# First four V loads in pieces of four tokens, spread by 0/1 matmuls, in a kernel of linear attention and an MLP

## The chip, the cores and the metric

The kernel runs on one core of a Trainium2 chip. The metric is the time of one execution on the device in microseconds (us). A core has a matmul engine (TensorE, PE in the profile), three engines for elementwise work (VectorE = DVE, ScalarE = ACT, GpSimd = POOL), SyncE (SP), which here only issues transfers, and 16 DMA engines that move the data.

## The reference

```python
def _attn_ref(q, k, v, f_logit):            # B, H, S, D = 4, 8, 768, 48
    f = 1.0 / (1.0 + np.exp(-f_logit))
    state = np.zeros((B, H, D, D))
    for t in range(S):
        state = f[:, :, t, :, None] * state + np.einsum('bhd,bhe->bhde', k[:, :, t], v[:, :, t])
        y[:, :, t] = np.einsum('bhd,bhde->bhe', q[:, :, t], state)

def _moe_ref(x, w_in, w_out):               # x: 3072 x 384, w_in: 384 x 2048, w_out: 2048 x 384
    h = x @ w_in
    g = np.maximum(0.01 * h, h)
    return g @ w_out
```

A linear attention with a decay per token and channel gives y; y, with heads side by side, is the input x of two matrix products with a leaky ReLU between them. Inputs and the output are float32.

## The kernel before

The sequence is cut into chunks of 128 tokens. A unit is one chunk of one batch with all eight heads, 24 in all; units 0 to 3 are the first chunk of the four batches. Within a chunk the recurrence becomes matmuls: the logarithm of the decay is summed over the tokens by a matmul with a triangular matrix (`gate_pe`), its exponentials scale k (`em`) and q (`a`), and both are turned so that channels lie on partitions. `score_pe` multiplies them, `mask` keeps the lower triangle, `mix_pe` applies scores and carried state to V, and `state_pe` makes the new state. `y_out` copies the result, `x_pe` and `x_out` turn it, and then, for pairs of units, `up` (eight groups), `up_act` (leaky ReLU) and `down` (two halves) run the MLP. Up to the last units, attention of later units is worked in between the MLP of earlier ones.

The first four units take a path of their own (functions with `q_`). f, k and q of the first chunk are loaded four tokens to a partition, in pieces of 768 bytes, and f of all four batches goes through exp (`q_exp_act`) and ln (`q_ln_act`) in two calls, one per half of the heads. `q_gate32` sums it by matmuls with 32 rows, `q_decay_b` takes exponentials, `q_turn_pe` turns k and q, and `q_k_mul` and `q_q_mul` multiply (half of the heads, pair of heads, pair of batches). `q_score_pe`, `q_wf_act` with `q_mask_pool` and `q_mask`, `q_mix_pe`, `q_back_pe` with `q_back_out` (k back to token partitions) and `q_state_dve` follow. V of these units is loaded in the ordinary way: one token to a partition, pieces of 192 bytes, cast by `cast_v`.

The order of all work is written out by hand, step by step, and every engine takes its steps in that order. SP issues nearly all loads, stores and DMA transposes (`turn2_dma` turns k and q of two units, `x2_dma` turns x of two units, for the pairs in `X2`); POOL issues the loads of w_in and w_out. A one-element copy on POOL (`touch`) makes POOL wait until a load has landed. `idle_pe` runs matmuls on a tile of zeros. Eight PSUM banks serve every step; the last number of a step is its bank.

Of the kernel before, what the change touches and what calls it, by code (L numbers as in the profile page):

```python
# [16 lines left out]
def kernel(  # L17
# [89 lines left out]
    nc.vector.memset(fill, 0.0)  # L107
    lfq = [const.tile([128, 4, 4, 64], BF16, name=f"lfq{i}", tag=f"lfq{i}") for i in range(2)]
# [62 lines left out]
    def load_part(u, name, src):  # L171
        c, b = units[u]
        t = raws[f"{name}_raw"][u % R_RAW]
        nc.sync.dma_start(out=t, in_=src[b, :, c * C:(c + 1) * C, :].rearrange("h t d -> t h d"))
        raw.setdefault(u, {})[name] = t
# [24 lines left out]
    X2 = (9, 10, 11)  # L200
# [23 lines left out]
    emT, aT = wide(gTs[GBUFS - 1]), wide(gTs[GBUFS - 2])  # L224
    kTq = [const.tile([128, 2, 4, 128], BF16, name=f"kTq{i}", tag=f"kTq{i}") for i in range(2)]
# [92 lines left out]
    def q_state_pool(b):  # L318
        put_state(b)
# [195 lines left out]
    load_part(0, "v", v)  # L515
    q_exp_act(1)
    load_part(1, "v", v)
    idle_pe(24, 7)
    q_gate32(0, 0, 1, 2, 3)
    touch('k')  # L520
    q_k_cast(V, 0)
    q_ln_act(1)
    q_k_cast(G, 1)
    q_turn_pe(khq, 0, 4)
    load_part(2, "v", v)
    q_decay_b(0, aT, -1.0, 0, 0)
    q_gate32(1, 0, 1, 2, 3)
    q_decay_b(1, emT, 1.0, 1, 0)
    load_w_in(0)
    q_decay_b(0, emT, 1.0, 0, 0)  # L530
    q_decay_b(2, emT, 1.0, 2, 0)
    q_turn_pe(khq, 1, 5)
    q_k_mul(0, 1, 0, 4)
    q_decay_b(1, aT, -1.0, 1, 0)
    load_w_in(1)
    q_decay_b(2, aT, -1.0, 2, 1)
    q_k_mul(0, 0, 0, 4)
    q_decay_b(1, emT, 1.0, 1, 1)
    load_part(3, "v", v)
    q_q_cast(V, 1)  # L540
    q_decay_b(3, emT, 1.0, 3, 1)
    q_decay_b(0, emT, 1.0, 0, 1)
    q_q_cast(V, 0)
    idle_pe(6, 7)
    q_turn_pe(qhq, 1, 6)
    q_decay_b(0, aT, -1.0, 0, 1)
    load_part(4, "f", f_logit)
    cast_v(G, 0)
    q_decay_b(1, aT, -1.0, 1, 1)
    q_k_mul(1, 0, 0, 5)  # L550
    q_turn_pe(qhq, 0, 7)
    q_decay_b(2, aT, -1.0, 2, 0)
    q_k_mul(1, 1, 0, 5)
    q_decay_b(2, emT, 1.0, 2, 1)
    q_q_mul(1, 0, 0, 6)
    q_decay_b(3, aT, -1.0, 3, 1)
    cast_v(G, 1)
    idle_pe(1, 1)
    q_back_pe(1, 0)
    q_q_mul(1, 1, 0, 6)  # L560
    q_decay_b(3, aT, -1.0, 3, 0)
    q_back_pe(0, 1)
    q_q_mul(0, 0, 0, 7)
    q_decay_b(3, emT, 1.0, 3, 0)
    q_back_out(A, 0, 1)
    q_q_mul(0, 1, 0, 7)
    idle_pe(2, 2)
    q_score_pe(1, 0, 2, 3)
    q_back_out(V, 1, 0)
    q_q_mul(1, 0, 1, 6)  # L570
    q_score_pe(0, 0, 1, 0)
    q_wf_act(1, 0, 1, 3)
    q_mask(1, 0, 0, 2)
    state_pe(1, 3)
# [24 lines left out]
    q_q_mul(0, 0, 1, 7)
    idle_pe(5, 1)  # L600
    q_score_pe(1, 1, 1, 3)
    q_k_mul(0, 1, 1, 4)
    up(0, 2, 5)
    q_mask(1, 1, 0, 1)
    q_wf_act(1, 1, 1, 3)
    q_back_pe(3, 2)
    up(0, 1, 6)
    up_act(0, 2, 5)
    q_mask_pool(1, 1, 1)
    q_back_out(V, 3, 2)  # L610
    up(0, 0, 0)
    up_act(0, 1, 6)
    q_score_pe(0, 1, 7, 4)
    up_act(0, 0, 0)
    up(0, 3, 3)
    q_mask(0, 1, 0, 7)
    q_wf_act(0, 1, 1, 4)
    load_part(4, "q", q)
    cast_v(G, 2)
    q_back_pe(2, 1)  # L620
    up_act(0, 3, 3)
    load_w_out(0)
    q_back_out(V, 2, 1)
    idle_pe(1, 0)
    up(0, 4, 5)
    load_part(4, "v", v)
    cast_v(V, 3)
    q_mask_pool(0, 1, 1)
    state_pe(2, 2)
    up(0, 5, 6)  # L630
    up_act(0, 4, 5)
    load_w_out(1)
    q_state_dve(2)
    load_part(5, "f", f_logit)
    q_mix_pe(2, 0)
    state_pe(3, 4)
    up_act(0, 5, 6)
    q_mix_pe(3, 7)
    y_out(V, 2, 0)
    q_state_pool(2)  # L640
    up(0, 7, 3)
    y_out(A, 3, 7)
    q_state_dve(3)
    load_part(5, "k", k)
    gate_exp(4)
    up(0, 6, 1)
    up_act(0, 7, 3)
    q_state_pool(3)
    x_pe(3, 5)
    x_pe(2, 2)  # L650
    gate_ln(4)
    x_out(V, 3, 5)
    x_out(A, 2, 2)
    load_w_out(2)
    up_act(0, 6, 1)
    idle_pe(4, 4)
    gate_pe(4, 6)
    load_w_out(3)
    up(1, 0, 0)
    decay_em(4, 6)  # L660
    decay_a(4, 6)
    up(1, 5, 7)
    k_scale(V, 4)
    up_act(1, 0, 0)
    up(1, 1, 4)
    up_act(1, 5, 7)
    up(1, 2, 3)
    up_act(1, 1, 4)
    load_part(5, "q", q)
    up(1, 6, 5)  # L670
    up_act(1, 2, 3)
    up(1, 3, 2)
    q_scale(V, 4)
    up_act(1, 6, 5)
    up(1, 4, 1)
    up_act(1, 3, 2)
    down(1, 0, 6)
    up_act(1, 4, 1)
    down(3, 0, 0)
    load_part(5, "v", v)  # L680
    turn_pe(4, 7)
    up(1, 7, 4)
    turn_k(A, 4, 7)
    turn_q(V, 4, 7)
    load_part(6, "f", f_logit)
    cast_v(G, 4)
    down(1, 1, 6)
    up_act(1, 7, 4)
    load_part(6, "k", k)
    gate_exp(5)  # L690
    state_pe(4, 3)
    score1_pe(4, 5, 2)
    gate_ln(5)
    put(V, 1, 6)
    load_part(6, "q", q)
    down(0, 0, 1)
    state_dve(4)
    mask(4, 0, 5)
    load_part(6, "v", v)
    gate_pe(5, 7)  # L700
    down(0, 1, 1)
    mask(4, 1, 2)
    decay_em(5, 7)
    load_part(7, "f", f_logit)
    cast_v(G, 5)
    decay_a(5, 7)
    k_scale(V, 5)
    mix_pe(4, 4)
    q_scale(G, 5)
    put(A, 0, 1)  # L710
    load_part(7, "k", k)
    down(2, 0, 6)
    gate_exp(6)
    y_out(V, 4, 4)
    state_pool(4)
    gate_ln(6)
    out_dma(1)
    turn_pe(5, 3)
    down(2, 1, 6)
    turn_k(A, 5, 3)  # L720
    turn_q(V, 5, 3)
    load_part(7, "q", q)
    load_part(7, "v", v)
    x_pe(4, 5)
    cast_v(V, 6)
    gate_pe(6, 2)
    put(A, 2, 6)
    load_part(8, "f", f_logit)
    state_pe(5, 7)
    x_out(V, 4, 5)  # L730
    score1_pe(5, 1, 4)
    decay_em(6, 2)
    state_dve(5)
    down(3, 1, 0)
    decay_a(6, 2)
    k_scale(G, 6)
    gate_exp(7)
    mask(5, 1, 4)
    out_dma(0)
    gate_ln(7)  # L740
# [648 lines left out]
```

## Time and profile before

| | |
|---|---|
| median of 3 runs | 181.87 us (181.64 to 181.93) |
| profiled execution, whole | 182.43 us |
| its span, first to last instruction | 180.7 us |
| mean granted clock of PE | 0.989 |
| busy: PE, DVE, ACT, POOL | 171.3, 87.0, 123.4, 54.8 us |
| matmuls of `up` (L466), `down` (L486) | 64.5, 65.9 us |
| DMA | 112,582 packets, 31.31 MB |

Rows of the timeline give the start and length of an instruction or of several alike (xN), its engine and line, what it writes and reads, and in brackets the idle time before it with what ended it. L142 is `idle_pe`, L150 and L148 are casts and copies of many kinds (DVE and ACT), told apart by their tiles. PEld is the loading of weights, which runs beside matmuls.

### The profile page before, as it was taken

What the parts mean: (1) busy time and instruction counts of PE and PEld (TensorE: products, weight loads), DVE (VectorE), ACT (ScalarE), POOL (GpSimd) and SP (SyncE); (2) the same over time, 40 slices, a digit from 0 to 9 for tenths busy, and PEclk for the clock granted to TensorE, in tenths of its full rate; (3) what the DMA queues carried; (4) which work ended last, traced back from release to release, by engine and by line L of the source; (5) the groups of instructions that cost most, each with busy time, mean ns of one, the idle gap of its engine ahead of it and who ended that gap; (6) DMA issues with size and microseconds to landing.
All of it is one profiled execution on the core that took longest, in us unless ns stands there. A gap on an engine that the chain in (4) does not pass through costs nothing.

```text
span 180.7 us, 4845 instructions
## 1 busy us (share of the span) xinstructions
PE 171.3 (95%) x1912; PEld 137.7 (76%) x1912; DVE 87.0 (48%) x203; ACT 123.4 (68%) x268; POOL 54.8 (30%) x108
## 2 busy tenths in 40 slices
PE   7597899999999999979999999999999999999992
PEld 5375699776788889669778788788785696897872
DVE  7249954044765978176467365670750254100000
ACT  2577689546888998758779669578796382583711
POOL 3074453114455646330421804250532300000000
PEclk9969999999999999999999999999999999999999
DMA  5999999979988999999999999998999962050102
GB/s 151 303 221 192 211 173 228 210 157 202 219 188 180 193 173 199 169 209 254 163 192 218 185 206 144 249 186 172 234 207 205 201 180 44 5 131 0 44 25 109
DMA packets 112582, 31.31 MB, mean 173 GB/s; under 512 B 105008, under 2 KB 111280, under 8 KB 112560
## 3 DMA queue, kind: packets, MB, share of 16 engines
q1 hardware_dynamic: 110640, 27.47, 79.7%
q0 software_dynamic: 1376, 3.15, 9.5%
q10 hardware_dynamic: 544, 0.39, 0.8%
q8 instruction: 15, 0.25, 0.6%
q14 instruction: 7, 0.06, 0.1%
HBM read 25.17 MB, written 4.72 MB: 165 GB/s over the span
## 4 chain that ended last, share of the span: by engine, by line
PE 54%; ACT 0%; issue 0%
PE ps L466 24%; PE ps L486 22%; PE ps L404 2%; PE ps L425 2%; PE ps L491 1%; PE ps L422 1%; PE ps L332 1%; PE ps L456 1%; PE ps L433 1%; PE ps L335 0%; ACT osb L148 0%
## 5 line engine op out<-in xcount | busy, mean ns | idle before, releaser
L486 PE MATMUL ps<-w_out_b,gT 128*128 128x384 bf16 x368 | 65.9, 326 | 0.0
L466 PE MATMUL ps<-xT,w_in 128*128 128x256 bf16 x528 | 64.5, 273 | 1.0 <-DVE xT L150 1.0
L471 ACT ACTIVATE gT<-ps 128x512 bf16<-128x512 f32 x88 | 51.7, 601 | 15.0 <-PE ps L466 12.9
L466 PEld LDWEIGHTS <-w_in 128*128 128x128 bf16 x528 | 56.0, 114 | 3.0 <-issue 1.1
L486 PEld LDWEIGHTS <-gT 128*128 128x128 bf16 x368 | 34.5, 98 | 19.8
L415 DVE TENSOR_TENSOR wm<-ps,ut 128x512 bf16<-128x512 f32 x40 | 25.2, 683 | 13.2 <-PE ps L404 11.6
L148 ACT COPY osb<-ps 128x384 f32<-128x384 f32 (+1 forms) x24 | 11.2, 466 | 21.2 <-PE ps L486 17.3
L316 POOL CAST sb<-sf 64x192 bf16<-64x192 f32 x40 | 14.6, 364 | 22.4 <-PE ps L422 18.9
L358 POOL TENSOR_TENSOR kqh<-q_raw,a_t 128x384 bf16<-128x384 f32 x11 | 10.1, 920 | 20.1 <-ACT a_end L344 6.8
L150 DVE CAST xn<-ps 128x384 bf16<-128x384 f32 x15 | 8.3, 556 | 7.6 <-PE ps L425 4.5
L354 POOL TENSOR_TENSOR kqh<-k_raw,em_t 128x384 bf16<-128x384 f32 x7 | 6.4, 918 | 17.6 <-ACT em_t L339 13.3
L354 DVE TENSOR_TENSOR kqh<-k_raw,em_t 128x384 bf16<-128x384 f32 x13 | 8.6, 658 | 6.6 <-ACT em_t L339 6.3
L339 ACT ACTIVATE em_t<-ps 128x384 bf16<-128x384 f32 x20 | 10.0, 498 | 2.0 <-PE ps L335 1.9
L323 ACT ACTIVATE f_raw<-f_raw 128x384 f32<-128x384 f32 x20 | 10.6, 530 | 1.0 <-DMA f_raw<-in_f_logit_dram 1.0
L150 POOL CAST v_b<-v_raw 128x384 bf16<-128x384 f32 x11 | 6.5, 588 | 15.8 <-DMA v_raw<-in_v_dram 15.8
L326 ACT ACTIVATE lf<-f_raw 128x384 bf16<-128x384 f32 x20 | 10.5, 526 | 0.3
L142 PE MATMUL ps<-fill 128*128 128x256 bf16 x46 | 9.3, 364 | 1.3 <-DVE fill L107 1.3
L342 ACT ACTIVATE a_t<-ps 128x384 bf16<-128x384 f32 x20 | 9.9, 495 | 0.8 <-PE ps L335 0.5
L358 DVE TENSOR_TENSOR kqh<-q_raw,a_t 128x384 bf16<-128x384 f32 x9 | 5.8, 644 | 7.2 <-ACT a_t L342 6.8
L150 DVE CAST v_b<-v_raw 128x384 bf16<-128x384 f32 x13 | 6.5, 503 | 5.3 <-DMA v_raw<-in_v_dram 5.2
L447 POOL TENSOR_TENSOR sf<-sf,a_end 128x192 f32<-128x192 f32 x16 | 8.8, 549 | 0.4
L441 DVE TENSOR_TENSOR sf<-sf,ps 64x192 f32<-64x192 f32 x16 | 5.5, 343 | 5.2 <-PE ps L433 1.8
(83 smaller groups left out, 192.6 us busy)
## 6 DMA issues: line engine op xcount, KB each, us to landing
v_raw<-in_v_dram SPq DMA_DIRECT2D x24, 192.0 KB, 4.4
out_dram<-osb SPq DMA_DIRECT2D x23, 192.0 KB, 3.2
f_raw<-in_f_logit_dram SPq DMA_DIRECT2D x20, 192.0 KB, 4.3
k_raw<-in_k_dram SPq DMA_DIRECT2D x20, 192.0 KB, 4.3
q_raw<-in_q_dram SPq DMA_DIRECT2D x20, 192.0 KB, 4.4
w_in<-in_moe_w_in_dram POOLq DMA_DIRECT2D x2, 768.0 KB, 10.8
w_out_b<-in_moe_w_out_dram POOLq DMA_DIRECT2D x4, 384.0 KB, 6.7
kq<-in_k_dram SPq DMA_DIRECT2D x4, 192.0 KB, 4.8
```

Of the source, the lines that this page charges most:

```text
L148: eng.copy(out=out, in_=in_)
L150: eng.tensor_copy(out=out, in_=in_)
L316: nc.gpsimd.tensor_copy(out=state_b[b][r, :, e * D:(e + 1) * D], in_=state_f[b][r])
L323: nc.scalar.activation(raw[u]["f"], raw[u]["f"], AF.Exp, scale=-1.0)
L326: nc.scalar.activation(lfs[u % R_LF][:, :, 0:D], raw[u]["f"], AF.Ln, bias=1.0)
L339: nc.scalar.activation(em_ts[u % R_EM], bank(bk)[:, 0:H * D], AF.Exp, scale=1.0)
L354: eng.tensor_mul(khs[u % R_KQS][:, :, 0:D], raw[u]["k"], em_ts[u % R_EM])
L358: eng.tensor_mul(qhs[u % R_KQS][:, :, 0:D], r["q"], a_ts[u % R_EM])
L415: nc.vector.tensor_mul(wms[e][u % R_WM], bank(bk).rearrange("p (i n) -> p i n", i=P2), ut[:, None, :].to_broadcast([128, P2, 128]))
L466: nc.tensor.matmul(bank(bk)[:, i * 256:(i + 1) * 256].rearrange("p (a n) -> p a n", a=2), w_in_p[ff // 8][:, kk, ff // 4 % 2, :, ff % 4], ...
L471: nc.scalar.activation(gTs[m % GBUFS][:, 2 * g:2 * g + 2].rearrange("p f a n -> p (f a n)"), bank(bk), AF.Prelu, alpha=0.01)
L486: nc.tensor.matmul(bank(bk)[:, 0:KD], g_part(u)[:, ff, :], w_out_b[:, ff, :], start=(ff == 0), stop=(ff == NF - 1))
```

## The change

V of the first four units is loaded as f, k and q are, four tokens to a partition, by `load_vq` into a tile of the MLP that is not yet in use. `q_v_cast` casts it on POOL, `q_pick` spreads it to one token per partition with a 0/1 matrix (`pick`, made on DVE at the start) by 16 matmuls of 32 rows and 384 columns, and `q_v_out` copies the result out of PSUM. The first loads of f go in halves, the first halves of all batches ahead of the second ones. x of units 16 and 17 (pair 8) is turned by a DMA transpose in place of six matmul transposes and two copies. The whole order of steps is new. In it w_in is loaded behind a `touch` of q, not of k, and its second half first; all four first units are finished up to their output before the first `up`; and exp and ln of unit 4's f (`gate_exp(4)`, `gate_ln(4)`) stand on ACT between casts of the first units.

```diff
-    first_load(nc.scalar, "f", 2)
-    first_load(nc.sync, "f", 0)
-    first_load(nc.sync, "f", 1)
-    first_load(nc.scalar, "f", 3)
+    first_load(nc.scalar, "f", 2, 0)
+    first_load(nc.sync, "f", 0, 0)
+    first_load(nc.sync, "f", 1, 0)
+    first_load(nc.scalar, "f", 3, 0)
+    first_load(nc.sync, "f", 0, 1)
+    first_load(nc.scalar, "f", 2, 1)
+    first_load(nc.sync, "f", 1, 1)
+    first_load(nc.scalar, "f", 3, 1)
...
+    vqb = const.tile([128, H, 4, D], BF16, tag="vqb")
...
-    X2 = (9, 10, 11)
+    X2 = (8, 9, 10, 11)
...
+    vq = gTs[GBUFS - 3].rearrange("p f a n -> p (f a n)").bitcast(FP32)[:, 0:H * 4 * D].rearrange(
+        "p (h j d) -> p h j d", h=H, j=4)
+    pick = gTs[GBUFS - 3].rearrange("p f a n -> p (f a n)")[:, 3072:3584].rearrange("p (i t j) -> p i t j", i=4, j=4)
+    nc.vector.memset(pick, 0.0)
+    eye = const.tile([128, 32], BF16, tag="eye")
+    for b in range(B):
+        r = slice(32 * b, 32 * b + 32)
+        nc.vector.tensor_copy(out=eye[r, :], in_=ident[r, r])
+    for i in range(4):
+        nc.vector.tensor_copy(out=pick[:, i, :, i], in_=eye)
+
+    def load_vq(b):
+        nc.sync.dma_start(out=vq[32 * b:32 * b + 32].rearrange("p h j d -> p h (j d)"),
+                          in_=v[b, :, 0:C, :].rearrange("h (t j) d -> t h (j d)", j=4))
...
+    def q_v_cast(eng, hh):
+        move(eng, vqb[:, 4 * hh:4 * hh + 4], vq[:, 4 * hh:4 * hh + 4])
+
+    def q_pick(bp, *bks):
+        for i in range(4):
+            for w in range(2):
+                b = 2 * bp + w
+                r = slice(32 * b, 32 * b + 32)
+                nc.tensor.matmul(bank(bks[w])[:, 0:H * D].rearrange("p (h d) -> p h d", h=H),
+                                 pick[r, i].rearrange("p t j -> p (t j)"), vqb[r, :, i, :],
+                                 start=(i == 0), stop=(i == 3))
+
+    def q_v_out(eng, b, bk):
+        move(eng, v_bs[b].rearrange("p h d -> p (h d)"), bank(bk)[:, 0:H * D])
```

The new order of the start, up to the first `up`, shortened (the engine is the first argument where there is one; V is DVE, A is ACT, G is POOL):

```
q_exp_act(0) q_ln_act(0) q_exp_act(1) idle_pe(24) q_gate32(0) q_ln_act(1) q_decay_b(1, emT, hh 0)
idle_pe(5) q_gate32(1) q_decay_b(0, emT, hh 0) q_k_cast(V, 0) q_k_cast(G, 1) load_vq(0)
q_decay_b(0, aT, hh 0) q_decay_b(1, aT, hh 0) q_turn_pe(k, 0) q_decay_b(1, aT, hh 1) load_vq(1) q_decay_b(2, aT)
q_turn_pe(k, 1) q_k_mul(0, 0, 0) load_vq(2) q_decay_b(3, emT) q_k_mul(0, 1, 0) q_decay_b(1, emT, hh 1) load_vq(3)
q_decay_b(2, emT) touch('q') q_q_cast(V, 0) load_part(4, "f") q_q_cast(A, 1) q_k_mul(1, 0, 1) load_w_in(1)
idle_pe(10) q_turn_pe(q, 0) ... q_k_mul(1, 1, 1) q_decay_b(0, emT, hh 1) q_k_mul(0, 0, 1) q_turn_pe(q, 1)
q_decay_b(0, aT, hh 1) load_w_in(0) ... q_k_mul(1, 0, 0) q_decay_b(3, aT) q_q_mul (0,0,0) (1,0,0) (1,1,1)
q_v_cast(G, 1) q_q_mul (1,0,1) (0,1,1) (1,1,0) q_v_cast(G, 0) q_k_mul(1, 1, 0) idle_pe(18) q_score_pe(1, 1)
q_q_mul(0, 1, 0) q_score_pe(1, 0) q_q_mul(0, 0, 1) q_wf_act(1, 1) q_pick(0) q_k_mul(0, 1, 1) q_wf_act(1, 0)
q_mask(1, 0) q_score_pe(0, 0) gate_exp(4) q_mask(1, 1) q_back_pe(0) q_v_out(A, 0) q_pick(1) q_mask(0, 0)
q_wf_act(0, 0) gate_ln(4) q_back_pe(3) q_back_out(V, 0) q_score_pe(0, 1) q_v_out(A, 3) q_v_out(V, 2) q_back_pe(1)
q_back_out(A, 3) q_v_out(V, 1) gate_pe(4) q_mix_pe(0) q_wf_act(0, 1) q_mask(0, 1) state_pe(0) q_mix_pe(1)
state_pe(3) y_out(A, 0) q_back_out(V, 1) q_back_pe(2) y_out(A, 1) q_state_dve(0) x_pe(0) q_back_out(A, 2)
state_pe(1) load_w_out(1) x_pe(1) q_mix_pe(2) x_out(A, 0) q_mix_pe(3) x_out(A, 1) state_pe(2) ... idle_pe(3) up(0, 6)
```

The steps after it are the same kinds as before in another order, with 61 fill matmuls in all where there were 46.

More of the change, by code (lines that the diff above doesn't have):

```diff
@@ L661 @@
[L661 to L668, printed above, removed]
+    q_decay_b(1, aT, -1.0, 1, 1)
+    load_vq(1)
+    q_decay_b(2, aT, -1.0, 2)
+    q_turn_pe(khq, 1, 5)
+    q_k_mul(0, 0, 0, 4)
+    load_vq(2)
+    q_decay_b(3, emT, 1.0, 3)
+    q_k_mul(0, 1, 0, 4)
+    q_decay_b(1, emT, 1.0, 1, 1)
+    load_vq(3)
+    q_decay_b(2, emT, 1.0, 2)
+    touch('q')
+    q_q_cast(V, 0)
+    load_part(4, "f", f_logit)
@@ new lines @@
+    mask(10, 0, 7)
+    q_scale(G, 14)
+    y_out(A, 11, 3)
+    cast_v(V, 14)
+    gate_exp(15)
+    state_pool(11)
+    mix_pe(10, 1)
+    gate_ln(15)
+    x_pe(11, 6)
+    state_pe(14, 0)
+    y_out(A, 10, 1)
+    down(7, 1, 2)
+    x_out(V, 11, 6)
+    load_part(15, "v", v)
+    state_pool(10)
+    load_part(16, "f", f_logit)
+    x_pe(10, 5)
+    gate_pe(15, 4)
+    put(A, 7, 2)
+    out_dma(8)
+    state_dve(14)
+    down(9, 0, 3)
+    x_out(A, 10, 5)
+    decay_em(15, 4)
+    decay_a(15, 4)
@@ new lines @@
+    up_act(5, 7, 6)
+    q_scale(V, 16)
+    load_part(17, "v", v)
+    state_pe(16, 7)
+    x_pe(12, 0)
+    load_part(18, "f", f_logit)
+    put(A, 9, 3)
+    down(10, 0, 2)
+    state_dve(16)
+    x_out(A, 12, 0)
+    load_part(18, "k", k)
+    up(6, 0, 1)
+    gate_exp(17)
+    load_part(18, "q", q)
+    up(6, 2, 5)
+    gate_ln(17)
+    up_act(6, 0, 1)
+    up(6, 7, 6)
+    load_part(18, "v", v)
+    up_act(6, 2, 5)
+    score_pe(7, 3, 0, 7, 1)
+    up_act(6, 7, 6)
+    gate_pe(17, 5)
+    out_dma(9)
@@ new lines @@
+    turn2_dma(8)
+    gate_pe(18, 3)
+    up(6, 4, 2)
+    up_act(6, 6, 1)
+    cast_v(V, 18)
+    decay_em(18, 3)
+    down(12, 0, 0)
+    decay_a(18, 3)
+    load_part(19, "v", v)
+    k_scale(V, 18)
+    up_act(6, 4, 2)
+    q_scale(G, 18)
+    state_pe(17, 6)
+    gate_exp(19)
+    down(11, 1, 4)
+    state_dve(17)
+    gate_ln(19)
+    state_pe(18, 7)
+    gate_pe(19, 5)
+    out_dma(10)
+    put(A, 11, 4)
+    x_pe(15, 1)
+    up(6, 5, 3)
+    decay_em(19, 5)
+    x_out(V, 15, 1)
+    decay_a(19, 5)
@@ new lines @@
+    put(A, 17, 4)
+    down(18, 0, 3)
+    down(19, 1, 5)
+    down(18, 1, 3)
+    out_dma(17)
+    put(A, 19, 5)
+    score_pe(11, 1, 0, 6, 2)
+    put(A, 18, 3)
+    up(10, 0, 7)
+    mask(23, 0, 6)
+    up(10, 5, 4)
+    mask(22, 1, 0)
+    up_act(10, 0, 7)
+    up(10, 2, 5)
+    mask(23, 1, 2)
+    up_act(10, 5, 4)
+    up(10, 3, 3)
+    out_dma(19)
+    mask(22, 0, 1)
+    up_act(10, 2, 5)
+    up(10, 1, 6)
+    up_act(10, 3, 3)
+    mix_pe(23, 7)
+    out_dma(18)
+    up_act(10, 1, 6)
+    mix_pe(22, 0)
@@ new lines @@
+    y_out(V, 23, 7)
+    up(10, 4, 4)
+    y_out(A, 22, 0)
+    down(20, 0, 2)
+    x2_dma(11)
+    up_act(10, 4, 4)
+    up(10, 6, 5)
+    up(10, 7, 1)
+    up_act(10, 6, 5)
+    down(21, 0, 3)
+    up_act(10, 7, 1)
+    down(20, 1, 2)
+    down(21, 1, 3)
+    put(A, 20, 2)
+    out_dma(20)
+    up(11, 0, 6)
+    put(A, 21, 3)
+    up(11, 2, 7)
+    up_act(11, 0, 6)
+    out_dma(21)
+    up(11, 6, 0)
+    up_act(11, 2, 7)
+    up(11, 3, 4)
+    up_act(11, 6, 0)
+    up(11, 5, 5)
+    up_act(11, 3, 4)
```

1343 lines of the change are left out of this document (605 added, 738 removed).

## The prediction

> **What bounds the kernel now.** I read the span and the stretches by engine first.
>
> ```profile
> span 180.7 us, 4845 instructions
> ```
> ```profile
> 20.98:77.80 56.82, 56.82 (x694) 46.57 (x692) 31.57 (x67) 45.06 (x102) 25.15 (x45) 1.00 1.05 191
> 77.80:79.20 1.40, 0.36 (x7) 0.27 (x4) 1.37 (x3) 0.48 (x1) 1.14 (x2) 1.00 0.92 198
> 79.20:177.50 98.30, 98.29 (x1022) 79.70 (x1020) 39.97 (x77) 65.15 (x136) 20.14 (x39) 1.00 0.82 156
> ```
>
> The first two numbers of a row are its length and PE's busy time. From 20.98, where the first `up` starts, to its last matmul at 177.5 PE is never idle but for 1.04 us. So the end is: start of the first `up`, plus a fixed amount of matmul work, plus holes, plus 3.2 us of last copy and store. The hole, in the timeline:
>
> ```profile
> 77.55 1.03 DVE L150 CAST v_b<-v_raw 128x384 bf16<-128x384 f32 x1 [1.61 <-DMA v_raw<-in_v_dram]
> 78.61 0.36 DVE L150 COPY xT<-ps 128x384 bf16<-128x384 bf16 x1
> 79.02 0.82 PE L466 MATMUL ps<-xT,w_in 128*128 128x256 bf16 x6 [1.04 <-DVE xT L150]
> ```
>
> A V cast waits for its late load, and the copy of x queued behind it on DVE lets PE stand. The change rewrites the whole order, so three things count: when the first `up` starts, how much work is left then, which holes come.
>
> **Work left.** In the new order units 2 and 3 are done up to their output before the first `up`; now much of them comes after it.
>
> ```profile
> 23.29 0.40 PE L277 MATMUL ps<-qTq,kTq 64*128 64x128 bf16 x8
> ...
> 24.30 0.39 PE L300 MATMUL ps<-ident,kTq 128*128 128x128 bf16 x4
> ...
> 24.52 0.27 PE L142 MATMUL ps<-fill 128*128 128x256 bf16 x1
> ...
> 26.11 0.36 PE L294 MATMUL ps<-v_b,wm 128*128 128x48 bf16 x8
> ...
> 26.32 0.33 PE L433 MATMUL ps<-v_b,kqh 128*128 128x96 bf16 x4
> ...
> 26.48 0.36 PE L294 MATMUL ps<-v_b,wm 128*128 128x48 bf16 x8
> ...
> 26.69 1.48 PE L466 MATMUL ps<-xT,w_in 128*128 128x256 bf16 x12
> ```
>
> Matmuls overlap, so starts count, not durations: turning back .22 (24.30 to 24.52), mix .21, state .16. Moved ahead are two each (1.18), one score block and the gate of unit 4 (estimated at .3 each): 1.8. Five fills (.11 each by 1.48/12 less the drain) vanish: .55. Six transposes of x 16 and 17 go to a DMA transpose: at .055 each (.22 for four) .33. That transpose has cover: its result is wanted 8 us of matmuls after unit 17's mix, so I cost it at nothing; a longer wait on SP would cost only what exceeds that. Left after the first `up`: 156.5 - 1.04 - 1.8 - .55 - .33 = 152.8. Hence span = first `up` + 152.8 + holes + 3.2, and a first `up` at 24.7 without holes breaks even.
>
> **The first `up`, step by step.**
>
> ```profile
> 0.81 0.89 SPq L70 DMA_DIRECT2D fq<-in_f_logit_dram  x2
> 1.74 2.67 SPq L70 DMA_DIRECT2D kq<-in_k_dram  x4
> 4.62 2.93 SPq L70 DMA_DIRECT2D qq<-in_q_dram  x4
> 6.44 0.84 ACT L229 ACTIVATE fq<-fq 128x768 f32<-128x768 f32 x1 [3.39 <-DMA fq<-in_f_logit_dram]
> 8.21 0.63 PE L240 MATMUL ps<-steps,lfq 32*128 32x128 bf16 x32 [1.74 <-ACT lfq L232]
> 9.67 0.37 ACT L245 ACTIVATE gT<-ps 128x256 f32<-128x256 f32 x1
> 9.99 1.73 POOL L190 DMA_DIRECT2D w_in<-in_moe_w_in_dram  x2
> 10.09 1.04 PE L240 MATMUL ps<-steps,lfq 32*128 32x128 bf16 x32
> 11.16 4.25 ACT L245 ACTIVATE gT<-ps 128x256 f32<-128x256 f32 x15 [1.12 <-PE ps L240]
> 14.18 1.41 DVE L263 TENSOR_TENSOR qTq<-ps,gT 128x256 bf16<-128x256 bf16 x4
> ```
> ```profile
> DMA to landing us min/median/max: 3.6/4.1/5.0
> ```
>
> *f in halves.* Loads of f land 3.6 to 5.0 after issue (last row); the last of four whole ones, issued near 1.3, releases ACT at 6.44. Four first halves are as many bytes as the first two whole loads, issued at .81 and landing by some 4.5. So exp starts at 4.6; bounds 4.3 and 5.6 (no gain in latency, 1.3 + 4.3). From exp to the first decay are 3.23 us (6.44 to 9.67): 7.8. Four more issues delay SP and ACT by some .9 each; ACT's table load still ends near 3.9, hidden. Only eight hardware loads can be open in the compiled program (each waits for the eighth before it), so k now waits for first halves of f to land, near 4.0 instead of 1.74. But k's bytes queued behind f's anyway, and q waited for f's landing already; I put q's landing unchanged, at 11.0, with +.6 as bound.
>
> *Decays.* The second gate block writes a bank that the first decay reads: it starts at 8.2 (7.8 + .37) and takes .63 or 1.04, the two rows L240. The trace slowed it:
>
> ```profile
> 5.00:10.00 5.00, 2.80 (x48) 1.74 (x47) 1.06 (x4) 3.50 (x5) 1.28 (x3) 0.97 1.10 309
> 9.70:13.00 3.30, 3.24 (x50) 2.50 (x47) 1.15 (x4) 2.18 (x9) 2.52 (x4) 0.50 1.38 211
> ```
>
> The granted clock (third from last) was .50 from 9.7 to 13, after 5 us in which PE was busy 2.80. The new order has 5 and 10 fills there. The Trainium skill, "TensorE: Matmul & The Clock Gate", Part 1, says that a free-running window of about 3.4 us decides; the trace agrees in that the slow stretch has about that length. By that rule the phase is luck, and half clock may fall elsewhere ahead of the first `up`. I take the full clock, .63, and +.4 as bound. DVE's new constants (about 1.3 us) are free: DVE was busy 1.06 of these 5 us.
>
> Decays run on ACT from 8.9 at 4.25/15 = .283 for 256 columns; eleven such widths precede the products of hh 1, batches 2 and 3: 12.0.
>
> *Products.* DVE does one each .353 (1.41/4). The eleventh, the last that score (1,0) needs, ends at 12.1 + 3.9 = 16.0; q's cast on DVE, 11.1 to 11.7, is not last, nor is the half on ACT. Score .40: 16.5.
>
> *ACT's list.* From there ACT has thirteen operations up to the second copy of x: three casts of scores, exp and ln of unit 4, two V copies, two copies of k, two of y, two of x.
>
> ```profile
> L281 ACT CAST wm<-ps 128x512 bf16<-128x512 f32 x4 | 2.3, 584 | 1.1 <-PE ps L277 1.1
> L148 ACT CAST xn<-ps 128x384 bf16<-128x384 f32 x2 | 0.9, 482 | 1.2 <-PE ps L294 1.2
> L148 ACT COPY kqh<-ps 128x512 bf16<-128x512 bf16 x1 | 0.8, 754 | 0.0
> ...
> L323 ACT ACTIVATE f_raw<-f_raw 128x384 f32<-128x384 f32 x20 | 10.6, 530 | 1.0 <-DMA f_raw<-in_f_logit_dram 1.0
> ...
> L326 ACT ACTIVATE lf<-f_raw 128x384 bf16<-128x384 f32 x20 | 10.5, 526 | 0.3
> ```
>
> 3 x .584 + 6 x .482 + 2 x .754 + .53 + .526 = 7.2, less some .04 of overlap at each: 6.7. DVE's masks and PE's steps between run beside it. First `up`: 23.2; bounds 22.6 and 24.3.
>
> *The spread of V.* The sixteen 0/1 matmuls (32 rows, 384 columns) fall before the first `up`, beside ACT's list. The nearest row, 32 gate matmuls of 32 rows and 128 columns in .63, gives .02 for 128 columns; 16 x 3 x .02 = .95 since there four row groups alternate and here two, up to 1.9 if that halves it. I take 1.3; against ACT's 6.7 it is hidden, and 1.9 would move the first `up` by perhaps .3. The Trainium skill, "TensorEngine Tiling (Array Packing)", Key Properties, speaks against it: a change of tiling mode drains the engine. No row here isolates a drain; by that rule a few of them, an estimated .3 us, would come on top.
>
> *Holes.* V of unit 13 will again be cast close to its load, but no x copy sits directly behind it. Following each other producer I find .4 us or more to spare; the new order is as tight, so I take .6 of holes, bounds 0 and 2.
>
> *Sum.* 23.2 + 152.8 + .6 + 3.2 = 179.8, .9 below the span of 180.7. The profiled execution took 182.43 as a whole; the runs' median is 181.87. Taking .9 off the median: 181.0.
>
> **Rivals.**
>
> *f of unit 4 blocks ACT (slower).* ACT's list holds exp of unit 4 ahead of V copies and score casts, and its load competes with w_in:
>
> ```profile
> q0 software_dynamic: 28, 0.06, 57.5%
> ...
> q0 software_dynamic: 626, 1.25, 95.9%
> q1 hardware_dynamic: 659, 0.12, 16.0%
> ```
> ```profile
> f_raw<-in_f_logit_dram SPq DMA_DIRECT2D x1, 192.0 KB, 13.1
> ```
> ```profile
> q1 hardware_dynamic: 1811, 0.34, 125.0%
> ```
>
> The first row is w_in's queue from 12.2 to 13.0, where its packets begin, 2.3 after its issue at 9.99. The next two are 14 to 21 us: 659 packets on SP's queue against w_in's 626, 94 a microsecond. The last row is 22 to 23.5, w_in done: 1,207 a microsecond. So the same load took 13.1 us in this stretch (middle). In the new order V's larger pieces go first, to 12.5, then the 1,024 packets of f, .85 us, done by 13.4; w_in is issued only when q has landed and a touch on POOL has run (estimated .6, from landing at 11.0), at 11.7, so it moves packets from 14.0. (Its first half, 384 packets at 626 in 7 us, is through by 18.3, the second by 22.6: in time for the first `up`.) ACT wants f at 17. Spared: .6. It decides from the point where w_in starts with over some 210 packets of f still to go. Half of them left: 5.4 us more, f at 20.2, 3.1 late, time 184; all left: up to 6 late, 187. Chance .12.
>
> *New holes (slower).* The new order may meet late loads, or a DMA transpose that holds SP, more often: 2.5 us of holes where I put .6 gives 182.9. For: the 16 DMA engines are full up to some 140 us (slices of 4.5 us, in tenths):
>
> ```profile
> DMA  5999999979988999999999999998999962050102
> ```
>
> Against: V's first four units have a quarter of the packets. Chance .16.
>
> *The start gains nothing (no change).* If half clock, whole-f latency or the spread put the first `up` at 24.2, the gain of the hole remains but is eaten by .6 of holes: 182.0. Chance .15.
>
> **How the numbers follow.** The forecast has .57. A measurement of this kernel can tell about 0.2%, .36 us. Faster .57 (first `up` plus holes below 24.3), the same .13, slower .30 (the two rivals and a little of the third). Range: 22.6 with no hole gives 178.6, thus 179.7; at the upper end 183.2 leaves out most late f's.
>
> **What would show it.** Right: exp at 4.6, decays from 8.9, last product near 17, first `up` near 23.2, PE busy from there to 175.9 + holes, no wait behind V of unit 13. Wrong: ACT idle before f of unit 4; a first `up` beyond 24.7; waits of PE above 1.5 us after it.

## The result, and the profile after

| | before | after |
|---|---|---|
| median | 181.71 us (181.23 to 183.52, 17 runs) | 183.66 us (182.44 to 186.11, 17 runs) |
| ratio, 95% interval | | 1.0083 (1.0054 to 1.0112) |
| profiled execution, span | 182.43, 180.7 us | 182.44, 180.7 us |

The change is slower, by some 1.5 to 2 us; 181.0 was forecast, with faster as the likeliest case. The ratios here and below leave out runs more than 1.5% above the fastest of their kernel (four of after, 185.28 to 186.11; one each of again, fill20 and v_behind; two of fill_qv, 184.06 and 184.21), which the medians and ranges keep. The two profiled executions are equally long and so don't show the loss by themselves: that of before was 0.7 us above the median of its runs here, and that of after was the fastest of its 17. The span of after, and two of its windows, in the columns of the prediction (the last is GB/s):

```profile
span 180.7 us, 4904 instructions
```
```profile
5.00:10.00 5.00, 3.06 (x77) 1.94 (x75) 1.76 (x12) 4.27 (x10) 0.00 (x0) 1.00 0.87 256
24.89:177.50 152.61, 152.42 (x1657) 124.17 (x1655) 67.58 (x139) 107.50 (x235) 43.51 (x81) 1.00 0.92 171
```

From the first `up` at 24.89 to its last matmul TensorE is busy for 152.42 of 152.61 us. So the fixed part came out as worked out (152.8), and all that is to be explained lies ahead of 24.89, where 23.2 had been forecast. The timeline of after up to there:

```profile
3.51 2.68 SPq L70 DMA_DIRECT2D kq<-in_k_dram  x4
4.31 0.84 ACT L250 ACTIVATE fq<-fq 128x768 f32<-128x768 f32 x1 [0.32 <-DMA fq<-in_f_logit_dram]
6.24 2.58 SPq L70 DMA_DIRECT2D qq<-in_q_dram  x4
8.65 2.96 ACT L266 ACTIVATE gT<-ps 128x256 f32<-128x256 f32 x8 [0.67 <-PE ps L261]
8.86 2.75 SPq L243 DMA_DIRECT2D gT<-in_v_dram  x4
10.31 0.56 DVE L155 CAST khq<-kq 128x768 bf16<-128x768 f32 x1 [3.47 <-DMA kq<-in_k_dram]
13.45 0.83 ACT L153 CAST qhq<-qq 128x768 bf16<-128x768 f32 x1 [1.84 <-DMA qq<-in_q_dram]
17.35 1.59 POOL L155 CAST vqb<-gT 128x768 bf16<-128x768 f32 x2 [1.56 <-DMA gT<-in_v_dram]
18.20 1.07 ACT L317 CAST wm<-ps 128x512 bf16<-128x512 f32 x2 [2.87 <-PE ps L313]
19.00 0.82 PE L283 MATMUL ps<-vqb,gT 32*128 32x384 bf16 x8 [0.55 <-POOL vqb L155]
19.16 0.54 ACT L359 ACTIVATE f_raw<-f_raw 128x384 f32<-128x384 f32 x1
24.89 0.82 PE L502 MATMUL ps<-xT,w_in 128*128 128x256 bf16 x6
```

f comes as planned: its first exp at 4.31, and the decays run from 8.65. Then three engines sit idle with a DMA in the brackets: DVE until k is there (10.31), ACT until q is (13.45), POOL until V is (17.35). Before, k's loads were issued at 1.74 and q's at 4.62; now at 3.51 and 6.24. What TensorE waited for, and the chain of waits back to the start (start, length, what):

```profile
PE ps L294 <- DVE khq L155: 2.3, 1, 2.3
PE ps L261 <- ACT lfq L253: 0.6, 2, 0.4
PE ps L283 <- POOL vqb L155: 0.5, 1, 0.5
```
```profile
0.81 2.69 DMA fq<-in_f_logit_dram
...
3.51 0.72 SPq L70
...
10.49 6.70 DMA gT<-in_v_dram
...
17.35 1.61 POOL vqb L155 x2
...
19.00 0.82 PE ps L283 x8
```

The chain starts at a landing of f: SP stands until 3.50, then issues k, q and V one after another, and the last of V's loads, issued at 10.49, takes 6.70 us. With eight loads of f, the first load of k is the ninth; it goes out when the first of the eight has landed. From 19.00, where the V spread begins, the chain is TensorE's own matmuls without a gap up to the first `up`.

### The profile page after: what moved, and what is told of

Same layout as the page of the kernel before. It is cut to its first block, busy times and chain, and to the rows that moved or that the text cites. A ratio compares the mean times of both kernels' runs of the same rounds, so it can differ in the third digit from the quotient of the medians.

```text
span 180.7 us, 4904 instructions
## 1 busy us (share of the span) xinstructions
PE 172.9 (96%) x1937; PEld 139.4 (77%) x1937; DVE 85.6 (47%) x211; ACT 124.0 (69%) x268; POOL 54.0 (30%) x105
## 4 chain that ended last, share of the span: by engine, by line
PE 86%; DMA 5%; SPq 4%; ACT 1%; issue 1%; POOL 1%; DVE 1%; POOLq 0%; DVEq 0%
PE ps L522 33%; PE ps L502 32%; DMA gT<-in_v_dram 4%; SPq L70 3%; PE ps L513 3%; PE ps L440 2%; PE ps L461 2%; PE ps L469 2%; PE ps L368 2%; PE ps L458 2%; DMA fq<-in_f_logit_dram 1%; PE ps L527 1%; PE ps L492 1%; PE ps L403 1%; POOL vqb L155 1%
## 5 line engine op out<-in xcount | busy, mean ns | idle before, releaser
L502 PE MATMUL ps<-xT,w_in 128*128 128x256 bf16 x528 | 62.9, 273 | 0.1
L507 ACT ACTIVATE gT<-ps 128x512 bf16<-128x512 f32 x88 | 51.1, 605 | 9.0 <-PE ps L502 6.9
L153 ACT COPY osb<-ps 128x384 f32<-128x384 f32 (+1 forms) x25 | 11.8, 473 | 22.4 <-PE ps L522 19.6
L394 POOL TENSOR_TENSOR kqh<-q_raw,a_t 128x384 bf16<-128x384 f32 x13 | 12.6, 967 | 28.3 <-ACT a_end L380 13.0
L147 PE MATMUL ps<-fill 128*128 128x256 bf16 x61 | 10.6, 340 | 1.3 <-DVE fill L111 1.3
L155 DVE CAST xn<-ps 128x384 bf16<-128x384 f32 x13 | 7.2, 557 | 8.1 <-PE ps L461 5.3
L147 PEld LDWEIGHTS <-fill 128*128 128x128 bf16 x61 | 7.2, 122 | 3.3 <-DVE fill L111 1.3
L155 POOL CAST v_b<-v_raw 128x384 bf16<-128x384 f32 x6 | 3.0, 504 | 20.8 <-DMA v_raw<-in_v_dram 20.8
L390 POOL TENSOR_TENSOR kqh<-k_raw,em_t 128x384 bf16<-128x384 f32 x5 | 4.9, 979 | 9.7 <-ACT em_t L375 9.7
```

The lines of the kernel that those rows point to most:

```text
L147: nc.tensor.matmul(bank(bk)[:, 0:256], fill[:, 0:128], fill[:, 0:256], start=True, stop=True)
L153: eng.copy(out=out, in_=in_)
L155: eng.tensor_copy(out=out, in_=in_)
L390: eng.tensor_mul(khs[u % R_KQS][:, :, 0:D], raw[u]["k"], em_ts[u % R_EM])
L394: eng.tensor_mul(qhs[u % R_KQS][:, :, 0:D], r["q"], a_ts[u % R_EM])
L502: nc.tensor.matmul(bank(bk)[:, i * 256:(i + 1) * 256].rearrange("p (a n) -> p a n", a=2), w_in_p[ff // 8][:, kk, ff // 4 % 2, :, ff % 4], ...
```

## Experiments

Theories at the start: (1) f in eight loads holds SP back, so that k, q and V land late; (2) half clock ahead of the first `up` costs the time; (3) V's loads themselves are slow. Rows are of one profiled execution of each kernel, times of five rounds against the kernel before on the same chip. There were four chips, on which the kernel before had medians of 181.25 to 181.48 us, so the ratios compare best. The columns q and V give the start of the first step that reads their landed data, with a dash where no step waits for it.

| kernel | q | V | first `up` | span less it | time, range | ratio, interval |
|---|---|---|---|---|---|---|
| before_again | – | – | 20.80 | 158.6 | 181.15, one run | |
| again | 14.77 | 18.75 | 26.30 | 155.7 | 183.7 (182.1 to 184.9) | 1.010 (1.0069 to 1.0131) |
| fill20 | 13.63 | 17.88 | 25.42 | 155.8 | 183.44 (182.4 to 185.4) | 1.010 (1.0069 to 1.0132) |
| f_whole | 11.91 | 15.80 | 24.01 | 156.0 | 181.83 (181.3 to 182.4) | 1.0024 (1.0009 to 1.0039) |
| h1_pool | 13.29 | 17.15 | 24.70 | 156.0 | 182.28 (181.9 to 183.0) | 1.0045 (1.0029 to 1.0061) |
| k_between | 13.32 | 17.44 | 25.93 | 155.8 | 182.96 (181.9 to 183.4) | 1.0078 (1.0051 to 1.0106) |
| v_spread | 11.07 | 13.62 | 24.24 | 156.0 | 181.7 (181.3 to 182.3) | 1.0012 (0.9991 to 1.0032) |
| v_spread_after | 12.76 | 15.33 | 23.36 | 156.0 | 181.43 (180.8 to 182.7) | 1.001 (0.9989 to 1.0032) |
| v_behind | 13.95 | 21.49 | 31.82 | 155.7 | 188.43 (186.5 to 189.6) | 1.0369 (1.0326 to 1.0411) |
| v_ordinary | 11.10 | – | 31.98 | 156.0 | 189.83 (189.1 to 190.1) | 1.0449 (1.0408 to 1.049) |
| touch_k | – | 15.37 | 24.06 | 155.9 | 181.69 (181.2 to 182.1) | 1.001 (0.9988 to 1.0031) |
| x_pe | 11.35 | 15.49 | 24.08 | 156.4 | 182.14 (181.7 to 182.5) | 1.0033 (1.0016 to 1.005) |
| f_whole_fill | 11.59 | 15.71 | 23.51 | 156.0 | 181.37 (181.0 to 181.6) | 0.9999 (0.9986 to 1.0012) |
| v_spread_fill | 10.86 | 13.40 | 23.57 | 155.9 | 181.25 (181.2 to 181.6) | 0.9998 (0.9987 to 1.0009) |
| fill_qv | 11.65 | 15.63 | 23.89 | 156.0 | 181.52 (181.2 to 184.2) | 1.0007 (0.9997 to 1.0018) |

Span less first `up` is 155.7 to 156.0 in every kernel that has the rest of the change (x_pe and before_again have another): the time is the first `up` plus a constant.

**again.** The changed kernel once more, unedited.

> The changed kernel unchanged, for its spread and a second profile. Clock theory: its runs fall into steps by mean granted clock, about 182.5 us at .99 to 1.0, 184 at .98, 185.4 at .972 (one, two, three windows of 3.4 us at half clock), and the kernel before stays near 181.7. Load theory (late loads at the start alone make the loss): times scatter without regard to the clock.

Its profiled execution took 183.72 us, a usual one. The rows of its timeline and waits that answer to those above, and its line by cores:

```profile
14.77 0.83 ACT L153 CAST qhq<-qq 128x768 bf16<-128x768 f32 x1 [3.02 <-DMA qq<-in_q_dram]
18.75 1.60 POOL L155 CAST vqb<-gT 128x768 bf16<-128x768 f32 x2 [1.65 <-DMA gT<-in_v_dram]
26.30 0.81 PE L502 MATMUL ps<-xT,w_in 128*128 128x256 bf16 x6
```
```profile
PE ps L294 <- DVE qhq L155: 2.4, 1, 2.4
PE ps L294 <- DVE khq L155: 1.8, 1, 1.8
PE ps L283 <- POOL vqb L155: 1.0, 1, 1.0
```
```profile
core 0: 182.0 us, clock 1.000
```

Issued at the same times as in after (q 6.24, V 8.87), q is read 1.3 us later and V 1.4 later, and the first `up` comes 1.4 later. The clock was full throughout, while after had this stretch (granted clock third from last):

```profile
10.00:15.00 5.00, 4.01 (x33) 3.17 (x34) 2.85 (x8) 3.16 (x8) 2.70 (x4) 0.70 1.04 225
```

From the reading of q to the first `up` after took 11.44 us and again 11.53, so the slow stretch does not show in the time. Nor do the runs of again fall into steps by their clock: 183.72 us came at 1.0 and 182.12 at .991. Half clock is not the loss: theory 2 falls.

**fill20.** Idle matmuls ahead of k's turning, to keep TensorE busy.

```diff
+    idle_pe(20, 7)
     q_turn_pe(khq, 0, 4)
```


> Twenty more fill matmuls on PE ahead of the turning of k, where PE stood 2.3 us; all else as changed. Clock theory: fewer windows at half clock, mean clock .99 to 1.0 in nearly all runs and the median 1 us or so lower, 182.4 to 182.8. Load theory: no gain, or .3 us slower, as fills can only delay the turning of k.

The clock of its profile stayed at 1.0, and the time did not move against that of again (183.44 and 183.7): TensorE waits for q and V at any clock.

**f_whole.** f in four whole loads; all else as changed.

```diff
-    first_load(nc.scalar, "f", 2, 0)
...
+    first_load(nc.scalar, "f", 2)
+    first_load(nc.sync, "f", 0)
+    first_load(nc.sync, "f", 1)
+    first_load(nc.scalar, "f", 3)
```


> f loaded in four whole loads again, all else as in the changed kernel. Load theory: k is issued near 1.75 instead of 3.51, q lands near 11 instead of 13.35 and V's pieces near 15 instead of 17.2, while exp starts at 6.4 instead of 4.3; products then wait for decays (13.8) instead of q (13.9), so the first up moves little, to 24.3 to 24.9. Time within 0.5 us of the changed kernel by that alone. Clock theory: PE no longer waits 2.3 us for k, so fewer half-clock windows and 1 us or more faster in the median.

```profile
1.74 2.68 SPq L70 DMA_DIRECT2D kq<-in_k_dram  x4
4.50 2.88 SPq L70 DMA_DIRECT2D qq<-in_q_dram  x4
6.27 0.84 ACT L246 ACTIVATE fq<-fq 128x768 f32<-128x768 f32 x1 [3.21 <-DMA fq<-in_f_logit_dram]
11.91 0.19 POOL L187 COPY seen<-qq 128x1 f32<-128x1 f32 x1 [2.19 <-DMA qq<-in_q_dram]
15.80 1.60 POOL L151 CAST vqb<-gT 128x768 bf16<-128x768 f32 x2 [1.49 <-DMA gT<-in_v_dram]
```

k goes out at 1.74 again, q at 4.50, and both q and V are there 1.5 to 3 us sooner than in the changed kernel's two profiles. f's exp starts 2 us later, and yet the time falls by 1.87 us against again, and the range of the runs from 2.8 to 1.0 us. Halving f, which was to bring exp 1.8 us forward, costs that much instead. This misses the expectation as written: late loads alone were to move the time by 0.5 us at most, and 1 us or more was to speak for the clock. But f_whole itself ran at half clock from 10 to 13 us (row below, under f_whole_fill) and again at no time, so the clock did not make this gain. Theory 1 stands, with a larger effect than I gave it.

**before_again.** The kernel before, profiled a second time.

> The kernel before, unchanged, for a second profile. If the hole of 1.04 us behind the cast of V of unit 13 belongs to every execution, PE waits about 1 us there again and the span is 180.4 to 180.7. If it was one execution's luck, the span is 179.2 to 180.1 with PE waiting under .3 us after its first up: the saving of 1.04 in the prediction was then not there to be had.

```profile
span 179.4 us, 4845 instructions
20.80:176.30 155.50, 155.30 (x1716) 126.47 (x1713) 72.40 (x145) 110.39 (x240) 46.71 (x85) 1.00 0.92 171
```

TensorE has no hole here. The 1.04 us behind V of unit 13 belonged to that one execution, not to the kernel. So what a first `up` of the changed kernel must beat is 179.4 - 156.0 = 23.4, not 24.7.

**h1_pool.** The second halves of f through POOL's queue, so that k need not wait.

```diff
+    for b in (0, 2, 1, 3):
+        first_load(nc.gpsimd, "f", b, 1)
```


> The second halves of f are loaded by POOL's queue, which does not count against the eight open loads; all else as changed. Load theory: exp still near 4.3, k issued near 1.75, k lands by 8.6, q by 11, V's pieces by 15; the first up comes at 23.2 to 23.8 instead of 24.89, so 1.1 to 1.7 us faster than the changed kernel's like runs, about 181.2 to 181.9. If the open loads do not matter, the first up stays at 24.9.

```profile
8.46 0.84 ACT L248 ACTIVATE fq<-fq 128x768 f32<-128x768 f32 x1 [2.41 <-DMA fq<-in_f_logit_dram]
```

k goes out at 1.73 and the first exp starts at 4.32, but the second halves, issued from 1.40 to 3.80, release the second exp only at 8.46, and q is read at 13.29. The first `up`, expected at 23.2 to 23.8, comes at 24.70. Of again's loss of 2.2 us 0.8 is left.

**k_between.** k of two batches between the halves of f.

```diff
+    first_load(nc.sync, "k", 0)
+    first_load(nc.sync, "k", 1)
     first_load(nc.sync, "f", 0, 1)
```


> The changed kernel with k of the first two units issued between the first and the second halves of f. If the loads wait for the one eight before them, the third of f's second halves is now the one that waits (at 3.5 us), k's first two go out at once, and q's four go out 0.9 us sooner, at about 5.3 instead of 6.24; the second exponential comes up to 1 us later. If q's landing sets the time through its issue: 182.6 to 183.0. If the second exponential takes over, or the bytes in flight set q's landing and not its issue: 183.4 to 184.

```profile
9.05 0.84 ACT L250 ACTIVATE fq<-fq 128x768 f32<-128x768 f32 x1 [3.00 <-DMA qq<-in_q_dram]
13.32 0.19 POOL L191 COPY seen<-qq 128x1 f32<-128x1 f32 x1 [2.13 <-DMA qq<-in_q_dram]
```

As in the theory of the eighth load before, the wait now falls on a half of f, and q goes out at 5.71 instead of 6.24. But the second exp comes 3 us late, not 1, and q is read hardly sooner. The bracket names q; what exp reads is f, whose last half went out on SP near 3.9, and the longest landing of a half was 5.1 us. 182.96 lies in the range of the first expectation, but not by its mechanism: one wait was exchanged for another.

**v_spread and v_spread_after.** V's pieces to every fourth partition, as k and q go, with whole f and with f in halves. V of the first four units is then in the wrong order of tokens.

```diff
-        nc.sync.dma_start(out=vq[32 * b:32 * b + 32].rearrange(
+        nc.sync.dma_start(out=vq[slice(b, None, 4)].rearrange(
```


> On the kernel with f loaded whole: V's pieces go to every fourth partition of the tile, as those of k and q do, in place of 32 neighbouring ones, so V of the first units comes out in a wrong order; all else equal. If the 32 neighbouring partitions slow V's packets, these take about 41 ns in place of 67 to 79, V's pieces land by 13.5 to 14 instead of 15.7, unit 4's f by 16 and the time falls by up to .3 us, to 181.5. If the slowing has another cause (queues, other traffic), V lands at 15.5 to 16 again and the time stays at 181.8.

Packets, MB and share of SP's queue from 10 to 12 us, and V's loads with their median from issue to landing, first of f_whole, then of v_spread:

```profile
q1 hardware_dynamic: 534, 0.39, 113.7%
```
```profile
gT<-in_v_dram SPq DMA_DIRECT2D x4, 192.0 KB, 5.7
```
```profile
q1 hardware_dynamic: 883, 0.64, 107.5%
```
```profile
gT<-in_v_dram SPq DMA_DIRECT2D x4, 192.0 KB, 3.8
```

With the engines about equally full, a packet takes 1.7 times as long with V going to 32 neighbouring partitions as with V spread; the last of q's packets are in the stretch too. With whole f the time hardly moves (181.7), since V is there before TensorE asks.

> The changed kernel with its f in halves, and V's pieces sent to every fourth partition, as k and q go, instead of 32 neighbouring ones (V of the first four units then comes in the wrong order of tokens). Theory A, that V's slow packets beside q's are what holds q back and spreads the time: in the kernel with whole f the same edit brought V's landing from 5.7 to 3.8 us behind its issue and q's packets in the stretch 10 to 12 us from 534 to 883. Here q would be cast at 12.5 to 13.0 instead of 13.4 to 14.8, V at 15 instead of 17.4 to 18.8, the first `up` at 24.2 and the time 182.4 with a spread under 1 us. Theory B, that the series of issues on SP alone, 1.77 us late, sets q's landing: q cast at 13.4 or later, the time 183.6 with the old spread.

```profile
12.76 0.83 ACT L153 CAST qhq<-qq 128x768 bf16<-128x768 f32 x1 [1.12 <-DMA qq<-in_q_dram]
15.33 1.59 POOL L155 CAST vqb<-gT 128x768 bf16<-128x768 f32 x2 [0.23 <-DMA gT<-in_v_dram]
23.36 0.82 PE L502 MATMUL ps<-xT,w_in 128*128 128x256 bf16 x6
```

With f in halves the same edit takes off 2.3 us against again. The two profiles, both at full clock, add up: q read 2.0 us sooner and TensorE's 1.0 us of waiting for V gone, against 2.94 at the first `up`. So theories 1 and 3 hold together, and the loss needs both parts: k and q issued late (k by 1.77 us), and V's slow loads right behind q. The first `up` and the time came out better than expected (24.2 and 182.4). The spread of runs stayed at 1.9 us, where under 1 was expected.

**v_behind.** V's loads behind f and k of unit 4 instead of right behind q.

```diff
     load_part(4, "k", k)
+    load_vq(0)
+    load_vq(1)
+    load_vq(2)
+    load_vq(3)
```


> The changed kernel, f in halves, with V's four pieces issued behind f and k of unit 4 instead of right behind q. If V's packets hold q back, q is now cast by 12.9 us (13.4 to 14.8 in the changed kernel, 12.8 where V went to spread partitions); V itself lands 1 to 2 us later, at 18.5 to 20. If q's landing is what costs the time, 182.5; if V's own landing ends the chain, the 0/1 matmuls wait until 20 to 21.5 us and the time is 184 to 185.5, slower than the changed kernel.

```profile
13.95 0.83 ACT L153 CAST qhq<-qq 128x768 bf16<-128x768 f32 x1 [2.26 <-DMA qq<-in_q_dram]
21.49 1.59 POOL L155 CAST vqb<-gT 128x768 bf16<-128x768 f32 x2 [5.20 <-DMA gT<-in_v_dram]
23.13 1.46 PE L283 MATMUL ps<-vqb,gT 32*128 32x384 bf16 x8 [4.56 <-POOL vqb L155]
```

q, at 13.95, lies between the changed kernel's two profiles (13.45 and 14.77), with the ordinary loads of unit 4 now behind it. So it is not V alone that holds q back; only V spread out gave 12.76. V itself is 2.7 us later than in again, more than expected. TensorE waits 4.6 us for it and then runs at half clock, so that eight matmuls of the V spread take 1.46 us where they took .82. The time, 188.43, is beyond the 184 to 185.5 expected.

**v_ordinary.** Whole f, V in pieces of 192 bytes as before, no 0/1 matmuls.

```diff
-    load_vq(0)
+    load_part(0, "v", v)
...
-    q_v_out(A, 0, 7)
+    cast_v(A, 0)
```


> On the kernel with f loaded whole: V of the first four units loaded in the ordinary way (1024 pieces of 192 bytes each) and cast where the spread's copies stood; no 0/1 matmuls. If V in larger pieces pays, this is slower: 4096 packets at about 900 a microsecond ahead of unit 4's f and w_in, V landed only by 16 to 23 where w_in's packets alternate, first up 1 to 4 us later, 183 to 186. If the spread costs more than the pieces save, it is faster than 181.8.

ACT's longest wait:

```profile
ACT f_raw L355 <- DMA f_raw<-in_f_logit_dram: 5.9, 1, 5.9
```

189.83, beyond the 183 to 186 expected: f of unit 4 is caught behind w_in, the prediction's first rival, and the first `up` comes at 31.98. From 14 to 17 us w_in's queue moved 227 packets and SP's 96. Half clock follows the wait (.50 from 25 to 31 us) and is in the 8 us that the larger pieces of V are worth in this order.

**touch_k.** Whole f; w_in behind k instead of q.

```diff
-    touch('q')
+    touch('k')
```


> On the kernel with f loaded whole: POOL's touch reads k in place of q, so w_in's load starts some 2 us earlier (10.3 in place of 12.5). By the prediction's first rival w_in's packets then alternate with unit 4's f from 12.6 on, f lands at 19 to 22.5 in place of 16.5 to 17, ACT waits for it 1 to 4 us with the casts of the first units behind it, and the time is 182.8 to 186. If w_in and f do not disturb each other, 181.8.

```profile
9.87 1.73 POOL L191 DMA_DIRECT2D w_in<-in_moe_w_in_dram  x2
```
```profile
DMA packets 1785, 1.12 MB, mean 223 GB/s; under 512 B 412, under 2 KB 1785, under 8 KB 1785
q1 hardware_dynamic: 1785, 1.12, 114.3%
```

w_in is issued at 9.87 and not at 12.45, but from 9 to 14 us all 1785 packets belong to SP's queue. The loss that I expected did not come, and the time is that of f_whole.

**x_pe.** Whole f; x of units 16 and 17 turned by TensorE again.

```diff
-    X2 = (8, 9, 10, 11)
+    X2 = (9, 10, 11)
...
-    x2_dma(8)
     put(A, 13, 6)
+    x_pe(16, 7)
+    x_out(V, 16, 7)
+    x_pe(17, 6)
+    x_out(V, 17, 6)
```


> f in whole loads, and x of units 16 and 17 transposed by TensorE as in the kernel before, with two copies out by VectorE; all else as with whole f. The prediction's term says that the six transposes cost 2 x 0.165 us of a TensorE that has no gaps there: 182.1 against 181.8 with the DMA transpose. If they fit beside VectorE's or ScalarE's work, or the DMA transpose itself costs as much elsewhere, the two are equal within 0.1.

Span less first `up` is 156.4 here and 156.0 with the DMA transpose, so the profile has the term (0.33) at 0.4. The intervals of the times overlap (1.0033 and 1.0024); by them alone it is not settled.

**f_whole_fill, v_spread_fill and fill_qv.** Whole f and 12 more idle matmuls ahead of the first widths; then the same with V spread (wrong order of tokens), and the same with q's second cast on DVE.

```diff
-    idle_pe(24, 7)
+    idle_pe(36, 7)
```
```diff
-    q_q_cast(A, 1)
+    q_q_cast(V, 1)
```


> f in whole loads and 12 more idle matmuls ahead of the first widths matmuls, where TensorE was idle for 1.48 us. If the half clock at 9.96 to 13.4 follows that idle time, the second group of widths matmuls takes 0.65 instead of 1.31 us, k's transposes 1.2 instead of 1.9, and the first `up` comes 0.3 to 0.8 us earlier than 24.0: 181.0 to 181.5, about the kernel before. If the products on VectorE and the exponentials on ScalarE set the chain and TensorE only waits, the first `up` stays at 24.0 and the time at 181.8.

The windows from 10 to 13 us, of f_whole and of f_whole_fill (granted clock third from last):

```profile
10.00:13.00 3.00, 3.00 (x49) 2.68 (x49) 0.96 (x3) 2.10 (x7) 0.74 (x2) 0.50 1.14 199
```
```profile
10.00:13.00 3.00, 2.97 (x64) 2.47 (x52) 1.22 (x3) 2.60 (x8) 1.06 (x2) 1.00 1.12 210
```

Here the clock does count: the first `up` comes at 23.51 instead of 24.01, the time falls to 181.37, level with the kernel before, and the runs lie within 0.65 us. The runs of f_whole say the same: the two of its twelve at a mean clock of 1.0 took 181.32 and 181.37, the others 181.63 to 182.36.

> Whole f, 12 more idle matmuls, V's pieces to every fourth partition (V of the first four units in the wrong order of tokens). Theory: with whole f, V has landed 2 us before TensorE asks for it, so the edit gives nothing: 181.4 as with neighbouring partitions, first `up` at 23.5. Rival: V's faster packets let everything behind them land sooner and show in the time: 181.0 or less.

181.25: nothing gained over f_whole_fill, as the theory had it. At full clock or near it, then, whole f gives 181.37 and 181.25 with V to neighbouring and to spread partitions, f in halves 183.44 (fill20) and 181.43.

> Whole f, 12 more idle matmuls, and the second cast of q by VectorE (0.55 us) instead of ScalarE (0.91 us at 13.16, between the exponentials that VectorE then waits for, 1.10 us). If ScalarE's list sets the first scores, they come 0.4 to 0.9 us sooner, the first `up` at 22.6 to 23.1 and the time is 180.5 to 181.0, below both kernels. If VectorE's products set them, 181.4 to 181.7.

```profile
16.57 0.46 PE L309 MATMUL ps<-qTq,kTq 64*128 64x128 bf16 x10 [0.78 <-DVE qTq L295]
17.57 0.34 PE L309 MATMUL ps<-qTq,kTq 64*128 64x128 bf16 x6 [0.54 <-DVE kTq L295]
```

A miss: TensorE now waits for DVE's products, and nothing is won.

No version beats the kernel before; f_whole_fill equals it.

## Why the prediction was wrong

**The step that failed** is in *f in halves*: "k's bytes queued behind f's anyway, and q waited for f's landing already; I put q's landing unchanged, at 11.0, with +.6 as bound". I had seen that k must wait for a landing of f (I put it near 4.0, measured 3.51), and then argued that the wait costs nothing because the transfer engines are full. They were not: from 5 to 10 us they moved 256 GB/s in after at a busy share of .87, where before had 309 at 1.10. And a late issue of k moves all that SP has behind it: q 1.6 us later than before, V after it. q was read at 13.45 and 14.77, V at 17.35 and 18.75 where I had its packets through by 12.5. f_whole takes the wait away, and with it all of the loss but 0.35 us.

**V's landing** was the second mis-sized term. Its last load took 6.70 us from issue to landing (chain of after). I had counted its packets as if nothing but their number mattered, and did not ask where the pieces go: 32 neighbouring partitions against every fourth. v_spread and v_spread_after show what that is worth, 0.1 us, within the noise, with whole f and 2.3 us with halves.

**The bar** was set wrong too. The 1.04 us hole was counted as the kernel's; before_again has none. With a first `up` at 23.2 and no holes my own sum gives 23.2 + 156.0 = 179.2 against 179.4, which is no gain that can be measured. v_spread_after reached 23.36 and came out level, as that says. From one execution I took its luck for structure, though the table said that it was 0.56 us above the median.

**What held.** Work left, 152.8 + 3.2: measured 155.7 to 156.0 in every kernel with the rest of the change. Exp at 4.6 (4.31), decays from 8.9 (8.65). The x transposes, .33 (0.4 in x_pe's profile). ACT's list was put at 6.7 and ran from 18.20 to 24.84, 6.6; but after 19.00 TensorE too was busy without a gap, so that this length is ACT's alone was not shown, and the agreement may be in part luck. The spread of V, taken at 1.3 within .95 to 1.9: two rows of .82, 1.64 together. Of the drain that the Trainium skill has in "TensorEngine Tiling (Array Packing)", Key Properties, no separate cost is seen in those two rows. Holes were put at .6 and were .2. Two last digits of the sums are off by .1, without effect (175.9 for 176.0, 179.7 for 179.8). f of unit 4 was in time (exp at 19.16 without a wait), though the mechanism is real, as v_ordinary shows with 5.9 us.

**The clock.** I took full clock, with half clock as bad luck. again ran at full clock and was slow; f_whole_fill gained 0.5 us at the first `up`. In f_whole, TensorE stood 1.48 us behind the 24 idle matmuls and the clock was half from 9.98 to 13.38; behind 36 it stood .73 and the clock stayed full. The Trainium skill, "TensorE: Matmul & The Clock Gate", Part 1, has a window of some 3.4 us, and the slow stretch of f_whole agrees with it in length. The clock was worth that only in the kernels in which no late landing set the pace.

**Of the rivals** none was what happened. *The start gains nothing* came nearest (24.2, 182.0), but by half clock or the spread; its size was short by the issue chain. The one on the slower side that I should have had is: k's wait passes to q and V, 1.8 us late on SP, from the point where q is read after the decays are ready.

**Left open.** What makes q land 1.3 us later in one execution of the same kernel than in another, with the same issue times; and why runs with f in halves still lie 1.9 us apart when V is spread.

## What to carry to other kernels

A load cut into pieces spends places among the loads that can be open; what stands behind it on the queue is late by a landing, and that has to be followed to every load behind, not only to the next one. Ask of each transfer into which partitions it writes, not only how large its pieces are. A single profile holds holes that are luck: compare its time with the median before counting them as a gain, and write the time as first step of the steady part plus a constant, which shows at once where a change can act.

## What I had not expected of the hardware

- With V's pieces of 768 bytes going to 32 neighbouring partitions, 534 packets moved in 2 us (f_whole), with every fourth partition 883 (v_spread); V's loads landed in 5.7 and 3.8 us.
- Loads given to POOL's queue between 1.40 and 3.80 us released their reader only at 8.46 us (h1_pool), and w_in, issued there at 9.87, moved no packet until 14 us while SP's queue was full (touch_k).
- Halving the loads of f brought its first exp 2 us forward (6.27 to 4.31) at the same total of bytes, and widened the spread of the runs from 1.0 to 2.8 us (again) and more.
